# Token-major x for the modulation by DMA transposes in three batches, with a new order of all steps

## The chip, the cores and the metric

The kernel runs on one core of a Trainium2 chip. The core has five engines with an instruction queue each: TensorE (PE), VectorE (DVE), ScalarE (ACT), GpSimd (POOL) and SyncE (SP, which here only issues DMAs). Sixteen DMA engines move data between HBM and SBUF for the core. Every engine works through its own queue in order and waits for semaphores of the others. The metric is the device time of one execution in microseconds (us).

## The reference, cut to what matters

Eight batches of attention (8 heads, 576 tokens, head width 64) are followed by a token and channel mixing block (576 tokens, width 512):

```python
# attention: a pooled part and a banded part, summed
q_d, k_d, v_d = mean of 4 tokens each              # 144 pooled tokens
out_d = softmax(q_d @ k_d.T / 8) @ v_d             # repeated 4 times along the tokens
out_l = softmax(where(|i - j| < 4, q @ k.T / 8, -1e9)) @ v
x = out_up + out_l                                 # [8, 576, 512]
# mixing block
theta = x @ w_theta
zr, zi = x * cos(theta), x * sin(theta)
y = w_tok_r @ zr + w_tok_i @ zi                    # over the tokens
u = x + y
out = u + relu(u @ w_ch)
```

Inputs and outputs are float32; the kernel computes in bfloat16 with float32 sums.

## The kernel before, in words

Each stage of one batch is a Python generator; every `yield` ends a step. A letter stands for a generator, and three strings, `FIRST`, `PERIOD` (three times) and `LAST` (L695 to L708), give the order in which steps of all batches are issued: the letter says whose next step comes. `pin()` (L713) ties each engine's instructions to that order, so the strings fix the order in every queue. A step is written here as letter, batch and number from zero: A3.1 is the second `turns` step of batch 3.

- L, `load`: DMAs of q, k and v, 11 steps in batches 0 and 1 and 9 in the others (3 of q, 3 of k, 3 of v). They land in eight float32 buffers of tag `st`, taken in turn. The small l loads the weights, some of them into the same eight buffers.
- C, `cast`: float32 to bfloat16 into `q_tm`, `k_tm` (one buffer each) and `v_w`, in the order of the loads. In batch 0, DVE casts q, ACT casts k and POOL casts v (L216); in all other batches POOL casts all. The small c casts weights.
- A, `turns`: TensorE transposes q and k to `qT`, `kT`. From batch 2 on there are twelve steps of four matmuls (L329); steps 0 and 1 read what C wrote first, 2 and 3 what it wrote next, and so on: step n needs C step n // 2. ACT copies the result, DVE the pooled columns. The last step of A makes the pooled v (`vd`), with two multiplications on POOL (L362).
- S, `scores`: two steps for the pooled part, five for the band. ACT takes exponentials; from batch 1 on POOL zeroes what is off the band with two `affine_select` on each band step (L442, L444).
- N, V: products with v, pooled (three steps) and banded (five). T: five steps that transpose to `xT` with channels on partitions, and add both parts.
- H, `phases`: theta on TensorE, sine and cosine on ACT, five steps. M, `last_product`: the last 64 tokens on DVE.
- Z, `modulate`: for each of four chunks of 128 tokens, four TensorE transposes (L581) bring x to tokens on partitions in PSUM, and one DVE multiplication (L582) makes `z`. The fifth step does the last 64 tokens.
- X, `mix`: eight steps of nine matmuls (L608), with a DVE addition each (L612). U, `residuals`: u with tokens on partitions by four DMA transposes (L621) in batches 1 to 6. R, `channels`: the product with w_ch. O, `store`: the last addition, on DVE, and the DMA to HBM.
- W turns the token weights, D is a block of six matmuls whose result nobody reads (L282).

All DMAs of L, l, U and O (but one) are issued by SP, in the order of the strings; one that must wait for a buffer or for a result keeps all later ones waiting. One-bank PSUM tiles (`w1`) go round four buffers and two-bank ones (`w2`) round two.

Of the kernel before, what the change touches and what calls it, by code (L numbers as in the profile page):

```python
# [9 lines left out]
FP32 = mybir.dt.float32  # L10
BF16 = mybir.dt.bfloat16
# [6 lines left out]
H = 8  # L18
# [29 lines left out]
def kernel(  # L48
# [38 lines left out]
    def load(b):  # L87

        if b < WIDE:
            for hh in range(4):  # L90
                for nm, src in zip("qk", (q, k)):
                    nc.sync.dma_start(
                        out=stage(b, f"{nm}{hh}")[0:TR, 0:2 * NTR * D].rearrange("p (h e) -> p h e", h=2),
                        in_=src[b, 2 * hh:2 * hh + 2].rearrange("h (p r) d -> p h (r d)", r=NTR),
                    )
                    yield
        else:
            for nm, src in zip("qk", (q, k)):
                for i in range(3):
                    t = stage(b, f"{nm}{i}")[0:TR].rearrange("p (c h d) -> p c h d", c=2, d=D)  # L100
                    for j in range(2):
                        c = 2 * i + j
                        nc.sync.dma_start(
                            out=t[:, j], in_=src[b, :, TR * c:TR * c + TR, :].rearrange("h p d -> p h d"),
                        )
                    yield
        for i in range(3):
            t = stage(b, f"v{i}").rearrange("p (c h d) -> p c h d", c=2, d=D)
            for c in range(2 * i, min(2 * i + 2, NCH)):
                nc.sync.dma_start(  # L110
                    out=t[0:KW[c], c % 2],
                    in_=v[b, :, KS[c]:KS[c] + KW[c], :].rearrange("h p d -> p h d"),
                )
            yield

    def cast(b):

        q_tm = work.tile([TR, NTR, H, D], BF16, tag="q_tm", bufs=1, name=f"q_tm{b}")
        k_tm = work.tile([TR, NTR, H, D], BF16, tag="k_tm", bufs=1, name=f"k_tm{b}")
        v_w = v_ws[b % 2]  # L120
        inputs[b] = (q_tm, k_tm, v_w)
        eng = CASTS.get(b, CASTS[None])
        if b < WIDE:
            for hh in range(4):
                for i, dst in enumerate((q_tm, k_tm)):
                    eng[i](out=dst[:, :, 2 * hh:2 * hh + 2, :].rearrange("p r h d -> p h r d"),
                           in_=staged.pop((b, f"{'qk'[i]}{hh}"))[0:TR, 0:2 * NTR * D].rearrange(
                               "p (h r d) -> p h r d", h=2, d=D))
                    yield
        else:  # L130
            for i, dst in enumerate((q_tm, k_tm)):
                for c in range(3):
                    eng[i](out=dst[:, 2 * c:2 * c + 2].rearrange("p c h d -> p (c h d)"),  # L133
                           in_=staged.pop((b, f"{'qk'[i]}{c}"))[0:TR])
                    yield
        for i in range(3):
            t = staged.pop((b, f"v{i}")).rearrange("p (c h d) -> p c h d", c=2, d=D)
            n, rows = (2, P) if i < 2 else (1, KW[4])
            eng[2](out=v_w[0:rows, 2 * i:2 * i + n, :, 0:D], in_=t[0:rows, 0:n])  # L139
            yield  # L140
# [151 lines left out]
    def turns(b):  # L292
# [8 lines left out]
        def wide_turn(n, hh):  # L301
            tm, To = ((q_tm, qT), (k_tm, kT))[n]
            ps = w2(f"pstr{n}{hh}_{b}")
            for r in range(NTR):
                nc.tensor.matmul(
                    out=ps[:, r // 3, (r % 3) * TR:(r % 3) * TR + TR],
                    lhsT=tm[:, r, 2 * hh:2 * hh + 2, :], rhs=ip[:, 0:TR], start=True, stop=True,
                )
            (dve if n == 1 else act)(
                out=To[:, hh, :].rearrange("p (w k c) -> p w k c", k=2, c=3),  # L310
                in_=ps[:, :, 0:3 * TR].rearrange("p k (c w) -> p w k c", w=TR),
            )

            with nc.allow_low_precision(reason="sums are taken in float32 and rounded once"):
                if n == 0:
                    nc.vector.tensor_reduce(out=qdT[:, hh, :], in_=To[:, hh, :].rearrange("p (m j) -> p m j", j=4),
                           axis=AX.X, op=ALU.add)
                else:
                    nc.vector.tensor_reduce(out=kdP[:, hh, 0:4, 0:30],
                       in_=To[:, hh, 0:480].rearrange("p (g m j) -> p g m j", g=4, j=4),  # L320
                           axis=AX.X, op=ALU.add)
                    nc.vector.tensor_reduce(out=kdP[:, hh, 4, 0:24], in_=To[:, hh, 480:576].rearrange("p (m j) -> p m j", j=4),
                           axis=AX.X, op=ALU.add)

        def turn(n, c):
            tm, To = ((q_tm, qT), (k_tm, kT))[n]
            ps = w1(f"pstr{n}{c}_{b}")[:, 0:4 * TW].rearrange("p (hh w) -> p hh w", w=TW)
            for hh in range(4):
                nc.tensor.matmul(  # L329
                    out=ps[:, hh, :], lhsT=tm[:, c, 2 * hh:2 * hh + 2, :], rhs=ip, start=True, stop=True,  # L330
                )
            nc.scalar.copy(out=To[:, :, TR * c:TR * c + TR], in_=ps[:, :, 0:TR])  # L332
            if n == 0:
                dve(out=qdT[:, :, TP * c:TP * c + TP], in_=ps[:, :, TR:TW])
            elif c == 5:
                nc.scalar.copy(out=kdP[:, :, 4, 0:TP], in_=ps[:, :, TR:TW])
            else:
                for g in range(TP * c // 30, (TP * c + TP - 1) // 30 + 1):
                    lo, hi = max(TP * c, 30 * g), min(TP * c + TP, 30 * g + 30)
                    nc.scalar.copy(out=kdP[:, :, g, lo - 30 * g:hi - 30 * g],  # L340
                                   in_=ps[:, :, TR + lo - TP * c:TR + hi - TP * c])

        for i in range(8 if b < WIDE else 12):
            if b < WIDE:
                wide_turn(i % 2, i // 2)
            else:
                turn(i // 6, i % 6)
            yield
# [23 lines left out]
    def scores(b):  # L372
# [3 lines left out]
        pd = pds[b] = work.tile([P, H + 2, SD], BF16, tag="pd", name=f"pd{b}")  # L376
        pms[b] = []

        scale = SCL / 16.0 if b < WIDE else SCL

        def pooled_scores(dst, hh):
            for par in range(2):
# [152 lines left out]
            yield  # L535


    css = {}

    def phases(b):  # L540

# [24 lines left out]
    def last_product(b):  # L566
# [4 lines left out]
        )  # L571
        yield

    def modulate(b):

        xT = xTs[b]
        z = zs[b] = moep.tile([P, 9, DM], BF16, tag="z", name=f"z{b}")
        for c in range(4):
            x = w1(f"psxt{c}_{b}", BF16)[:, 0:DM].rearrange("p (e d) -> p e d", d=P)
            for dc in range(4):  # L580
                nc.tensor.transpose(out=x[:, dc, :], in_=xT[:, dc, P * c:P * c + P], identity=ident)  # L581
            nc.vector.tensor_tensor(  # L582
                out=z[:, 2 * c:2 * c + 2, :].rearrange("p r (e d) -> p r e d", d=P),
                in0=x.unsqueeze(1).to_broadcast([P, 2, 4, P]),
                in1=css.pop((b, c)).rearrange("p r (e d) -> p r e d", d=P), op=ALU.mult,
            )
# [80 lines left out]
    def store(b):  # L667
# [17 lines left out]
            yield  # L685


    DMA_U = (1, 2, 3, 4, 5, 6)

# [1 line left out]


    FIRST = (  # L695
        "LLLCCLCALLALLCCALACDLCLADACAlAlCSSSClCSLASlScDVlNCcNAlNlVcSDlLcccWcTCLTcVVLHTAZCLVCHTCWALWWWLLTLLCCA"
        "LCWZWAAHLLAHWHADLWCSLCCCMZCLLZASlZlLCXSXACANSAACXLCSLNAAAXNSSXVAccCAXTCALVAACVLXLSTTSSHLVVXLTLHCTZRO"
        "AHZZCLHVLROHRLLMCOCSZZCNRLROSLNALOA"
    )
    PERIOD = (  # L700
        "XSCSNTXCCAAXCUAAVAXUACVAXAVAAVXTSSTAXSTAUTHXULCNHZNCAHLZCVHHCZROLLSLMSZRLOZRORLOLROL"
    )
    PERIODS = 3
    LAST = (
        "ASXVAAAXAAVXACCNAVXAUTACCCSUTTXTASSCXAHXVZUNHCTHXCAUHZNHZSZLLLRCMOLARORSSCZLRSOOCCNAXAXACAVAAVXXAVTA"
        "XUSSTARVXSOSXASTTHVUXVTHUNHZUZHNZHRMOSSZRORZORVXSONXTVTXXTVHXVXUHTZXTZHZUUHXZHMURROZROOXXRORXOXXXXRO"
        "ROXRORORORO"
    )  # L708

    last = {}  # L710
# [13 lines left out]
    def batches(steps, bs=range(B)):  # L724
        for b in bs:
# [43 lines left out]
```

## Time and profile before

| | |
|---|---|
| median of 11 runs | 261.03 us (260.13 to 263.73) |
| the profiled execution | 261.55 us, its span 259.8 us |
| PE busy | 243.2 us of the span |
| DVE, ACT, POOL busy | 188.6, 178.7, 154.5 us |
| bytes moved | 46.73 MB, mean 180 GB/s |

The span goes from the first to the last instruction on the core. A line of the timeline or of the groups says start, length, engine, source line, operation and what it writes and reads; what stands in brackets is idle time before it and what ended it. In the slices a digit is the busy share of one fortieth of the span in tenths, 6.5 us a slice. The DMA share is the mean busy share of the sixteen DMA engines; overlapping packets can take it over 1. Durations of matmuls are modelled ends, so the cost of a matmul in a stream is read from the distance of the starts.

### The profile page before, as it was taken

What the parts mean: (1) busy time and instruction counts of PE and PEld (TensorE: products, weight loads), DVE (VectorE), ACT (ScalarE), POOL (GpSimd) and SP (SyncE); (2) the same over time, 40 slices, a digit from 0 to 9 for tenths busy, and PEclk for the clock granted to TensorE, in tenths of its full rate; (3) what the DMA queues carried; (4) which work ended last, traced back from release to release, by engine and by line L of the source; (5) the groups of instructions that cost most, each with busy time, mean ns of one, the idle gap of its engine ahead of it and who ended that gap; (6) DMA issues with size and microseconds to landing.
All of it is one profiled execution on the core that took longest, in us unless ns stands there. A gap on an engine that the chain in (4) does not pass through costs nothing.

```text
span 259.8 us, 7472 instructions
## 1 busy us (share of the span) xinstructions
PE 243.2 (94%) x2960; PEld 170.1 (65%) x2960; DVE 188.6 (73%) x421; ACT 178.7 (69%) x336; POOL 154.5 (59%) x178
## 2 busy tenths in 40 slices
PE   1869699999999999999999999999999999999993
PEld 1434466678657877588657866687668766776762
DVE  4865869956768777868696868785777588876443
ACT  3439378997889678956896779777886787334022
POOL 4244364489997979398748956798069762600000
PEclk9985679999999999999999999999999999999999
DMA  7999999999999951999789987898399032311324
GB/s 191 247 246 318 278 248 202 198 276 224 191 244 219 265 119 27 204 226 271 109 172 218 287 141 145 191 264 209 52 245 243 23 63 81 105 40 43 143 74 150
DMA packets 120851, 46.73 MB, mean 180 GB/s; under 512 B 110448, under 2 KB 114544, under 8 KB 120816
## 3 DMA queue, kind: packets, MB, share of 16 engines
q1 hardware_dynamic: 120736, 46.18, 80.7%
q8 instruction: 23, 0.38, 0.6%
q14 instruction: 12, 0.10, 0.1%
q10 hardware_dynamic: 80, 0.07, 0.1%
HBM read 33.65 MB, written 9.44 MB: 166 GB/s over the span
## 4 chain that ended last, share of the span: by engine, by line
PE 85%; ACT 5%; DVE 5%; DMA 2%; issue 1%; SPq 0%; DVEq 0%
PE psu L608 27%; PE psr L632 11%; PE psth L546 10%; PE pstr L329 6%; PE psS L421 4%; PE psloc L498 4%; PE wu L282 3%; PE psxt L581 3%; PE xTps L528 3%; DMA st_k<-in_k_dram 2%; PE psnd L460 2%; PE psr L650 2%; PE pstl L557 1%; ACT pm L429 1%; PE psnd L466 1%; PE psxd L483 1%
## 5 line engine op out<-in xcount | busy, mean ns | idle before, releaser
L608 PE MATMUL psu<-WT,z 128*128 128x288 bf16 x576 | 80.0, 286 | 0.0
L608 PEld LDWEIGHTS <-z 128*128 128x128 bf16 x576 | 53.6, 98 | 15.2 <-issue 0.8
L442 POOL TENSOR_SCALAR_AFFINE_SELECT pm<-pm 128x1024 bf16<-128x1024 bf16 (+1 forms) x35 | 36.7, 1047 | 22.9 <-ACT pm L429 22.8
L612 DVE TENSOR_TENSOR uT<-psu,xT 128x288 bf16<-128x288 f32 x64 | 29.2, 456 | 24.2 <-PE psu L608 23.3
L429 ACT ACTIVATE pm<-psS 128x1024 bf16<-128x1024 f32 (+1 forms) x40 | 38.1, 984 | 10.7 <-PE psS L421 10.5
L444 POOL TENSOR_SCALAR_AFFINE_SELECT pm<-pm 128x1024 bf16<-128x1024 bf16 (+1 forms) x35 | 36.7, 1049 | 2.4
L546 PE MATMUL psth<-wth,xT 128*128 128x512 bf16 x128 | 32.9, 379 | 0.4 <-DVE xT L529 0.4
L632 PE MATMUL psr<-wch,uT 128*128 128x512 bf16 x128 | 32.0, 380 | 0.0
L551 ACT ACTIVATE cs<-psth,pihc 128x512 bf16<-128x512 f32 x32 | 22.0, 688 | 11.8 <-PE psth L546 8.0
L529 DVE TENSOR_TENSOR xT<-xTps,xdT 128x480 bf16<-128x480 bf16 (+1 forms) x40 | 24.9, 631 | 5.8 <-PE xTps L528 5.2
L507 DVE TENSOR_TENSOR tmp<-psloc,rl 120x512 bf16<-120x512 f32 (+1 forms) x40 | 27.6, 690 | 1.4
L139 POOL CAST v_w<-st_v 128x1024 bf16<-128x1024 f32 (+1 forms) x24 | 20.8, 897 | 11.3 <-DMA st_v<-in_v_dram 11.3
L582 DVE TENSOR_TENSOR z<-psxt,cs 128x1024 bf16<-128x1024 bf16 x32 | 21.7, 685 | 4.7 <-PE psxt L581 3.1
L133 POOL CAST k_tm<-st_k 96x1024 bf16<-96x1024 f32 x18 | 18.8, 1045 | 8.8 <-DMA st_k<-in_k_dram 8.2
L332 ACT CAST kT<-pstr 128x384 bf16<-128x384 f32 x36 | 18.0, 500 | 7.0 <-PE pstr L329 6.9
L662 ACT ACTIVATE rel<-psr 128x512 f32<-128x512 f32 (+1 forms) x16 | 7.9, 492 | 18.5 <-PE psr L650 15.0
L133 POOL CAST q_tm<-st_q 96x1024 bf16<-96x1024 f32 x18 | 18.4, 1035 | 1.9 <-DMA st_q<-in_q_dram 1.9
L332 ACT CAST qT<-pstr 128x384 bf16<-128x384 f32 x36 | 16.0, 481 | 4.9 <-PE pstr L329 4.7
L552 ACT ACTIVATE cs<-psth 128x512 bf16<-128x512 f32 x32 | 18.9, 590 | 0.0
L673 DVE SCALAR_TENSOR_TENSOR osb<-psr,utm 128x512 f32<-128x512 f32 x24 | 16.3, 687 | 2.4 <-PE psr L632 1.9
L632 PEld LDWEIGHTS <-uT 128*128 128x128 bf16 x128 | 11.2, 98 | 9.8
L498 PE MATMUL psloc<-v_w,pm 128*128 128x65 bf16 (+1 forms) x320 | 17.3, 198 | 0.0
(107 smaller groups left out, 439.5 us busy)
## 6 DMA issues: line engine op xcount, KB each, us to landing
st_v<-in_v_dram SPq DMA_DIRECT2D x32, 256.0 KB, 5.2
out_dram<-osb SPq DMA_DIRECT2D x32, 256.0 KB, 3.7
st_q<-in_q_dram SPq DMA_DIRECT2D x36, 192.0 KB, 4.8
st_k<-in_k_dram SPq DMA_DIRECT2D x36, 192.0 KB, 3.9
st_q<-in_q_dram SPq DMA_DIRECT2D x8, 288.0 KB, 6.0
st_k<-in_k_dram SPq DMA_DIRECT2D x8, 288.0 KB, 11.3
st_v<-in_v_dram SPq DMA_DIRECT2D x8, 200.0 KB
w<-in_moe_w_tok_r_dram SPq DMA_DIRECT2D x2, 576.0 KB
```

What stands on the lines that cost most here:

```text
L133: eng[i](out=dst[:, 2 * c:2 * c + 2].rearrange("p c h d -> p (c h d)"), in_=staged.pop((b, f"{'qk'[i]}{c}"))[0:TR])
L332: nc.scalar.copy(out=To[:, :, TR * c:TR * c + TR], in_=ps[:, :, 0:TR])
L429: nc.scalar.activation(out=pv, in_=ps[0:kw].rearrange("p e (j w) -> p (e j) w", w=P)[:, :, 0:qn], func=AF.Exp, scale=SCL,)
L442: nc.gpsimd.affine_select(out=pv, in_=pv, compare_op=ALU.is_ge, fill=0.0, base=off, pattern=[[0, 8], [-1, qn]], channel_multiplier=1)
L444: nc.gpsimd.affine_select(out=pv, in_=pv, compare_op=ALU.is_ge, fill=0.0, base=6 - off, pattern=[[0, 8], [1, qn]], channel_multiplier=-1)
L498: nc.tensor.matmul(out=pv[0:qn, par, j, :], lhsT=pms[b][c][0:kw, 4 * par + j, 0:qn], rhs=v_w[0:kw, c, 2 * j + par, 0:65], start=(j == 0), ...
L507: nc.vector.tensor_tensor(out=tmp[0:cnt].rearrange("p (j e d) -> p e j d", e=2, j=4), in0=pv[0:cnt, :, :, 0:D], in1=rl[0:cnt].unsqueeze(3) ...
L529: nc.vector.tensor_tensor(out=xT[:, :, QS[c]:QS[c] + cnt].rearrange("p e (m j) -> p e m j", j=4), in0=ps[:, :, 0:cnt].rearrange("p e (m j) ...
L546: nc.tensor.matmul(out=th, lhsT=xT[:, dc, P * c:P * c + P], rhs=wth[:, dc, :], start=(dc == 0), stop=(dc == 3),)
L608: nc.tensor.matmul(out=ps[:, 0:288], lhsT=z[:, j, P * dc:P * dc + P], rhs=WT[:, j, cols], start=(j == 0), stop=(j == 8),)
L612: nc.vector.tensor_tensor(out=uT[:, dc, cols], in0=ps[:, 0:288], in1=xT[:, dc, cols], op=ALU.add)
L632: nc.tensor.matmul(out=psr, lhsT=uT[:, dc, P * c:P * c + P], rhs=wch[:, dc, :], start=(dc == 0), stop=(dc == 3),)
```

## The change

In batches 5, 6 and 7, four DMA transposes a batch, issued by SP in a new step Y (`tokens`), write x with tokens on partitions to SBUF, and Z's first four steps multiply from there; their sixteen TensorE transposes a batch are gone. Y reads `xT` after T's last step. The buffer `x_tm` is there once, so Y of a batch waits for Z of the one before.

All three order strings are new. In `LAST` twelve Y steps are added. The number of steps in each section changes a little: `FIRST` has two C, one L and one S more and one N less, `LAST` the reverse. The strings also move the five D blocks, the weight loads and the loads of batch 1.

A second part of the diff, for turning q and k by DMA in batches of a list `DMA_A`, is off: that list is empty, and with it those lines do what they did before. The only trace of it is that `q_tm` and `k_tm` have 128 partitions in place of 96.

```diff
+    def tokens(b):
+
+        x = x_tm[b] = moep.tile([P, 4, 4, P], BF16, tag="xtm", bufs=1, name=f"xtm_{b}")
+        for dc in range(4):
+            nc.sync.dma_start_transpose(out=x[:, dc], in_=xTs[b][:, dc, 0:512])
+            yield
+
     def modulate(b):
 
         xT = xTs[b]
         z = zs[b] = moep.tile([P, 9, DM], BF16, tag="z", name=f"z{b}")
         for c in range(4):
-            x = w1(f"psxt{c}_{b}", BF16)[:, 0:DM].rearrange("p (e d) -> p e d", d=P)
-            for dc in range(4):
-                nc.tensor.transpose(out=x[:, dc, :], in_=xT[:, dc, P * c:P * c + P], identity=ident)
+            if b in DMA_X:
+                x = x_tm[b][:, :, c, :]
+            else:
+                x = w1(f"psxt{c}_{b}", BF16)[:, 0:DM].rearrange("p (e d) -> p e d", d=P)
+                for dc in range(4):
+                    nc.tensor.transpose(out=x[:, dc, :], in_=xT[:, dc, P * c:P * c + P], identity=ident)
             nc.vector.tensor_tensor(
...
-    DMA_U = (1, 2, 3, 4, 5, 6)
+    DMA_A, DMA_X, DMA_U = (), (5, 6, 7), (1, 2, 3, 4, 5, 6)
...
     FIRST = (
-        "LLLCCLCALLALLCCALACDLCLADACAlAlCSSSClCSLASlScDVlNCcNAlNlVcSDlLcccWcTCLTcVVLHTAZCLVCHTCWALWWWLLTLLCCA"
-        "LCWZWAAHLLAHWHADLWCSLCCCMZCLLZASlZlLCXSXACANSAACXLCSLNAAAXNSSXVAccCAXTCALVAACVLXLSTTSSHLVVXLTLHCTZRO"
-        "AHZZCLHVLROHRLLMCOCSZZCNRLROSLNALOA"
+        "LLLCCCLLAALLCCLLLAALAlClCCLLCAALLAlSCSlSCSlSAllLScCCVlDcVCLCSLcALNALcDDcCALcWcVDcNDAALWWCCLWWCLAAWSL"
+        "WALNWWLTCSCCVSlVTACSTSTHTLVNHNZHZHCZHNZLMCAAALAZAALCLlVCCASCCCTLXAXVAXAAACXTSLSXTASSXVLCALcAHVTNcHXT"
+        "LLHZHZCVHRCLZOLCSXMRRLLLSOOSZZCROLRCLO"
     )
     PERIOD = (
-        "XSCSNTXCCAAXCUAAVAXUACVAXAVAAVXTSSTAXSTAUTHXULCNHZNCAHLZCVHHCZROLLSLMSZRLOZRORLOLROL"
+        "SCNAAAXAVAXAXAAVCNVUCXCAAXASCSLUTTXATSSTCXAHVUXVTHUNZZHHRCLCOZLHMSSZRROLCOLZRLLLROLO"
     )
     PERIODS = 3
     LAST = (
-        "ASXVAAAXAAVXACCNAVXAUTACCCSUTTXTASSCXAHXVZUNHCTHXCAUHZNHZSZLLLRCMOLARORSSCZLRSOOCCNAXAXACAVAAVXXAVTA"
-        "XUSSTARVXSOSXASTTHVUXVTHUNHZUZHNZHRMOSSZRORZORVXSONXTVTXXTVHXVXUHTZXTZHZUUHXZHMURROZROOXXRORXOXXXXRO"
-        "ROXRORORORO"
+        "CAVAAASXCAVAANXACVAAXNSTCVAUTSCTTASSCXTYAANYSUYAAXAYSNHHXVVXAVZAHZNLUCCLHXUZHCMLZAVAASCZRLROOAXSCTXT"
+        "SSTTRVOAXSSTRYRYOUSOYNXYNXVVNXSHVVXZHXTHTTZHVHTZHRHUUUOZTYHRYRMYYOZOROXXRXOUXZZHHZZUMXXXZXXXXXRUUOXX"
+        "RXOROROROXRORROROROO"
     )
...
-                     M=batches(last_product), U=batches(residuals, DMA_U),
+                     M=batches(last_product), Y=batches(tokens, DMA_X), U=batches(residuals, DMA_U),
```

More of the change, by code (lines that the diff above doesn't have):

```diff
@@ L98, in load @@
             for nm, src in zip("qk", (q, k)):
+                rows = P if b in DMA_A else TR
                 for i in range(3):
[L100 to L105, printed above, removed]
+                    t = stage(b, f"{nm}{i}").rearrange("p (c h d) -> p c h d", c=2, d=D)
+                    for c in range(2 * i, 2 * i + 2):
+                        n = min(rows, S - rows * c)
+                        if n > 0:
+                            nc.sync.dma_start(
+                                out=t[0:n, c % 2], in_=src[b, :, rows * c:rows * c + n, :].rearrange("h p d -> p h d"),
+                            )
                     yield
@@ L116, in cast @@
     def cast(b):
-        q_tm = work.tile([TR, NTR, H, D], BF16, tag="q_tm", bufs=1, name=f"q_tm{b}")
-        k_tm = work.tile([TR, NTR, H, D], BF16, tag="k_tm", bufs=1, name=f"k_tm{b}")
+        q_tm = work.tile([P, NTR, H, D], BF16, tag="q_tm", bufs=1, name=f"q_tm{b}")
+        k_tm = work.tile([P, NTR, H, D], BF16, tag="k_tm", bufs=1, name=f"k_tm{b}")
         v_w = v_ws[b % 2]
@@ L125, in cast @@
                 for i, dst in enumerate((q_tm, k_tm)):
-                    eng[i](out=dst[:, :, 2 * hh:2 * hh + 2, :].rearrange("p r h d -> p h r d"),
+                    eng[i](out=dst[0:TR, :, 2 * hh:2 * hh + 2, :].rearrange("p r h d -> p h r d"),
                            in_=staged.pop((b, f"{'qk'[i]}{hh}"))[0:TR, 0:2 * NTR * D].rearrange(
@@ L132, in cast @@
                 for c in range(3):
-                    eng[i](out=dst[:, 2 * c:2 * c + 2].rearrange("p c h d -> p (c h d)"),
-                           in_=staged.pop((b, f"{'qk'[i]}{c}"))[0:TR])
+                    rows, n = (TR, 2) if b not in DMA_A else (P, 2) if c < 2 else (HALF, 1)
+                    eng[i](out=dst[0:rows, 2 * c:2 * c + n].rearrange("p c h d -> p (c h d)"),
+                           in_=staged.pop((b, f"{'qk'[i]}{c}"))[0:rows, 0:n * H * D])
                     yield
@@ L306, in wide_turn @@
                     out=ps[:, r // 3, (r % 3) * TR:(r % 3) * TR + TR],
-                    lhsT=tm[:, r, 2 * hh:2 * hh + 2, :], rhs=ip[:, 0:TR], start=True, stop=True,
+                    lhsT=tm[0:TR, r, 2 * hh:2 * hh + 2, :], rhs=ip[:, 0:TR], start=True, stop=True,
                 )
@@ L329, in turn @@
                 nc.tensor.matmul(
-                    out=ps[:, hh, :], lhsT=tm[:, c, 2 * hh:2 * hh + 2, :], rhs=ip, start=True, stop=True,
+                    out=ps[:, hh, :], lhsT=tm[0:TR, c, 2 * hh:2 * hh + 2, :], rhs=ip, start=True, stop=True,
                 )
@@ L341, in turn, with dma_turn @@
                                    in_=ps[:, :, TR + lo - TP * c:TR + hi - TP * c])
+        def dma_turn(n, c):
+            tm, To = ((q_tm, qT), (k_tm, kT))[n]
+            if c < 5:
+                rows = min(P, S - P * c)
+                nc.sync.dma_start_transpose(out=To[:, :, P * c:P * c + rows],
+                                            in_=tm[0:rows, c].rearrange("p h d -> p (h d)"))
+                return
+            x = To.rearrange("p e (m j) -> p e m j", j=4)
+            t = stg.tile([P, 1024], FP32, tag="st", name=f"sum{n}_{b}")[:, 0:4 * SD].rearrange("p (e m) -> p e m", m=SD)
+            add = nc.gpsimd.tensor_tensor
+            add(out=t, in0=x[:, :, :, 0], in1=x[:, :, :, 1], op=ALU.add)
+            add(out=t, in0=t, in1=x[:, :, :, 2], op=ALU.add)
+            if n == 0:
+                add(out=qdT, in0=t, in1=x[:, :, :, 3], op=ALU.add)
+            else:
+                add(out=kdP[:, :, 0:4, 0:30], in0=t[:, :, 0:120].rearrange("p e (g m) -> p e g m", g=4),
+                    in1=x[:, :, 0:120, 3].rearrange("p e (g m) -> p e g m", g=4), op=ALU.add)
+                add(out=kdP[:, :, 4, 0:24], in0=t[:, :, 120:SD], in1=x[:, :, 120:SD, 3], op=ALU.add)
         for i in range(8 if b < WIDE else 12):
-            if b < WIDE:
+            if b in DMA_A:
+                dma_turn(i // 6, i % 6)
+            elif b < WIDE:
                 wide_turn(i % 2, i // 2)
@@ L377, in scores @@
         pms[b] = []
-        scale = SCL / 16.0 if b < WIDE else SCL
+        scale = SCL / 16.0 if b < WIDE or b in DMA_A else SCL
         def pooled_scores(dst, hh):
@@ L535, in transposes @@
             yield
-    css = {}
+    css, x_tm = {}, {}
     def phases(b):
@@ L578, in modulate @@
         for c in range(4):
-            x = w1(f"psxt{c}_{b}", BF16)[:, 0:DM].rearrange("p (e d) -> p e d", d=P)
-            for dc in range(4):
-                nc.tensor.transpose(out=x[:, dc, :], in_=xT[:, dc, P * c:P * c + P], identity=ident)
+            if b in DMA_X:
+                x = x_tm[b][:, :, c, :]
+            else:
+                x = w1(f"psxt{c}_{b}", BF16)[:, 0:DM].rearrange("p (e d) -> p e d", d=P)
+                for dc in range(4):
+                    nc.tensor.transpose(out=x[:, dc, :], in_=xT[:, dc, P * c:P * c + P], identity=ident)
             nc.vector.tensor_tensor(
```

## The prediction

> **What bounds the kernel now.** I read the slices first, then the windows of the head, then POOL's timeline. The page:
>
> ```profile
> span 259.8 us, 7472 instructions
> ...
> PE   1869699999999999999999999999999999999993
> ...
> POOL 4244364489997979398748956798069762600000
> ...
> DMA  7999999999999951999789987898399032311324
> ```
>
> PE has no idle slice from about 45 us to the end, so every us of PE work taken out after that is a us of time. But the DMA engines too are full until slice 14, and the head decides when PE gets its work. By windows (columns: PE, PEld, DVE, ACT, POOL busy, clock, DMA share, GB/s):
>
> ```profile
> 30.00:47.00 17.00, 16.06 (x175) 10.57 (x173) 14.16 (x28) 13.92 (x22) 8.44 (x10) 0.85 1.10 221
> 47.00:60.00 13.00, 12.98 (x190) 9.29 (x186) 9.07 (x24) 12.15 (x23) 8.95 (x11) 1.00 1.12 246
> 60.00:70.00 10.00, 9.90 (x152) 7.64 (x149) 7.02 (x16) 8.05 (x19) 9.79 (x11) 1.00 1.16 207
> 70.00:83.80 13.80, 13.71 (x171) 8.93 (x169) 10.72 (x21) 12.29 (x21) 12.38 (x14) 1.00 1.12 223
> ```
>
> The DMA share is over 1 throughout, and from 54 us POOL too is full. POOL's timeline shows where it waits for a load and what each of its operations costs from start to start:
>
> ```profile
> 44.97 1.04 POOL L139 CAST v_w<-st_v 128x1024 bf16<-128x1024 f32 x1 [1.70 <-DMA st_v<-in_v_dram]
> 46.39 0.61 POOL L139 CAST v_w<-st_v 100x512 bf16<-100x512 f32 x1 [0.38 <-DMA st_v<-in_v_dram]
> 48.21 1.04 POOL L133 CAST q_tm<-st_q 96x1024 bf16<-96x1024 f32 x1 [1.20 <-DMA st_q<-in_q_dram]
> 49.94 1.04 POOL L133 CAST q_tm<-st_q 96x1024 bf16<-96x1024 f32 x1 [0.69 <-DMA st_q<-in_q_dram]
> 53.00 1.18 POOL L362 TENSOR_TENSOR vd<-last,own 128x256 bf16<-128x256 bf16 x2 [2.02 <-ACT last L360]
> 54.12 1.03 POOL L133 CAST q_tm<-st_q 96x1024 bf16<-96x1024 f32 x1
> 55.11 1.09 POOL L442 TENSOR_SCALAR_AFFINE_SELECT pm<-pm 128x1024 bf16<-128x1024 bf16 x1
> 56.27 1.09 POOL L444 TENSOR_SCALAR_AFFINE_SELECT pm<-pm 128x1024 bf16<-128x1024 bf16 x1
> 57.31 1.03 POOL L133 CAST k_tm<-st_k 96x1024 bf16<-96x1024 f32 x1
> ```
>
> POOL waits for the last v of batch 1 until 46.39 and is through at 47.0 (C1.10). A cast costs 1.0, the pair of selects of a band step 2.2 (55.11 to 57.31), vd 1.1.
>
> [...] four of L581 take 0.22 us between the starts around them. [...] L569, both inputs in SBUF, takes 0.91 at worst, 0.425 at the median. [...] The lines for what is moved:
>
> ```profile
> L621 SPq DMA_TRANSPOSE utm<-uT x24: 1190/1220/2420, 92.3 to 236.4; - x24
> DMA to landing us min/median/max: 2.3/2.8/4.7
> L582 DVE TENSOR_TENSOR z<-psxt,cs x32: 676/690/693, 39.6 to 236.3; 128x1024 bf16<-128x1024 bf16 x32
> L569 DVE TENSOR_TENSOR zl<-csl,xT x8: 411/425/908, 49.5 to 237.4; 128x512 bf16<-128x512 bf16 x8
> ```
>
> **The removed transposes.** 12 Z steps of four matmuls at 0.22 us: 2.64 us of PE work, all where PE is full. This is the whole direct gain. Nothing else is removed.
>
> **The added transposes.** Twelve on SP at 1.22 us of issue, the last landing 2.8 us after its issue starts: a batch's four need 3 x 1.22 + 2.8 = 6.5 us from T's last addition. In the new order of PE, Z's first step comes 8.5, 9.5 and 8.8 us of PE work after T's last step (batches 5, 6, 7). In batch 5 one U stands among the Ys (7.7 us against 8.5, less about 0.7 for T's addition), in batch 6 two stores and one U: tight but hidden behind S, X, A and V steps. I take 0; if all cover failed, half a us to one and a half a batch. DVE's 12 multiplications now read SBUF twice: 0.69 again (the 0.425 of L569 is for half the size[...]), and in batch 5, where POOL still works, up to 1.05 (a select) more each: 0 to 2 us of DVE, whose steps there, from X4.1 to C7.7, sum to 16.4 us beside 18.9 of PE. I take 0, hidden by the rest; with the cover gone 1 us.
>
> **The new order, head.** PE prices of the steps, from the distances of starts in its timeline: A 0.21 (0.26 in batches 0 and 1, last step 0.39); S 0.20, 0.39, then 0.33, 0.23, 0.28, 0.23, 0.25; N 0.50, 0.50, 0.27; V 0.24; T 0.21; H 0.86, last 0.47; Z 0.22, last 0.35; X 1.10; R 0.86 (1.08 in batches 0 and 7), last 0.67; W 0.45. Summed over the strings without D: 216.05 before, 213.41 after. From 72 us on the kernel before spends 182 us for 176 us of these, a factor of 1.033.
>
> All bytes needed before C1.10 are the same set in both orders (batches 0 and 1 and three weights, 10.9 MB), and the DMA side is full all that time, so C1.10 stays at 47.0, although D no longer delays A0.4 to A0.7 (which frees DVE some 2 us sooner: it only waits longer for batch 1). After it, POOL's new order is: S1.2, vd of A1.8, C2.0, S1.3, S1.4, C2.1 to C2.5, S1.5, C2.6 to C2.8, C3.0, S1.6, vd of A2.12, S2.2, C3.1. That is five full band steps (11.0), the short one (1.8), two vd (2.2), eight q and k casts (8.0), three v casts (2.6): 25.6, so C3.1 ends at 72.6 without a wait. One wait is to be seen: S1.5's exponential stands on ACT behind H0. From S1.4's end at 50.3 (47.0, then A1.8's copies and two exponentials): two table loads at 1.28, H0 at 4 x 1.17 + 0.85, six A2 copies at 0.42, one at 0.62, the exponential 0.93: 12.2, so 62.4, where POOL is free at 60.7. With it C3.1 ends at 74.3.
>
> PE's order needs C3.1 much earlier than it did. X0.0 stands behind A2.6, which needs C2.3, on POOL's list at 58.7; X0.0 starts near 59.7 (51.4 before), and A3.1, which needs C3.1, is reached 10.4 us of work later, at 70.4. There PE stops for 2.2 to 3.9 us, and behind A3.1 in its queue wait H1, N2, X0.6, and so all of ACT's and DVE's next work. At A3.1 the new order has 35.0 us of PE work done. The kernel before had 39.6 done at 72.6 and 41.0 at 74.3. Deficit 4.6 to 6.0, less the 2.64 saved: 2.0 to 3.4 us of work, times 1.033: 2.0 to 3.5. I take the middle, 2.8, since helpers ahead after the stop may win back some of the 0.6 us that PE loses between 74 and 84 before. Periods: same work, same 27.4 us; 0 to 0.4 us each either way.
>
> Sum on the profiled execution: 259.8 + 2.8 = 262.6 of span, 261.55 + 2.8 = 264.4; on the median of 261.03, which lies 0.5 lower, 263.8.
>
> **Rivals.** (1) Faster: loads are queued earlier now (theta, token weights and the first q and k of batch 1 stand ahead of S0), so if the DMA side had slack that its share hides, C1.10 comes earlier and so the whole POOL chain. For: in the windows from 28 to 36 us it moved 0.21 to 0.27 MB/us, and 0.36 when weights ran. Against: share over 1 throughout. The point from which it decides: the time is equal when A3.1 starts at 70.6 (before had 35.0 + 2.64 done then), so C1.10 must come 2 to 4 us earlier; the full saving needs C3.1 near 68, and gives 258.3. (2) No change: the chain runs 2 us ahead of my sum, PE is never stopped, and the late X0.0 eats just the saved 2.64: 261. (3) Slower by the tail: the transposes land late because SP, in order, waits for a store between them; DVE then waits in Z, and X behind it: 1 us a batch on top of the stop, 266.5. For: batch 5 has under 1 us of margin; against: 2 us in the others. That the change does nothing is no rival for Y; for the q and k part it is so by its empty list.
>
> **How the numbers follow.** The stop in the head, tail hidden: 0.52, 262.3 to 265.5, and 263.8 the likeliest. Rival 3: 0.14. Rival 2: 0.16. Rival 1: 0.18. Half a per cent (1.3 us) is about what a measurement of this kernel tells from none. Slower 0.66, same 0.16, faster 0.18. The range goes from 259.2, which leaves out most of rival 1, to 267.0.
>
> **What would show it.** PE idle of 2 us or more before the A3.1 matmuls of `q_tm` between 70 and 75 us, released by POOL's cast; X0.0 at 58 to 61; C1.10 ending at 46 to 48; PE free of L581 in the last three batches; DVE waits before Z under 0.5 us. Wrong would be: C1.10 before 45, periods that are not 27.4 us, or DVE waiting in Z for a transpose.

## The result, and the profile after

The changed kernel takes 265.38 us (median of 12 executions, 263.43 to 270.98) against 260.89 us of the kernel before (47 executions, 259.36 to 264.3); the ratio, which like all ratios below takes only the executions within 1.5% of each kernel's fastest, is 1.014 with an interval of 1.0109 to 1.0171. The change makes the kernel slower, by 1.4%. The profiled execution took 267.68 us, its span 266.0 us, 2.3 us above the median; its mean clock of PE was 0.971, where the twelve have 0.964 to 0.993 and a median of 0.976 (the clock is looked at below).

The page of the changed kernel, the same rows as of the kernel before:

```profile
span 266.0 us, 7391 instructions
...
PE   1369569998999999999999999999999999999993
...
POOL 4245425597698697939683978399965881000000
PEclk9999996579999999999999999999999999999998
DMA  7999997999998898399957996799689244375145
```

PE has its last idle slice (an 8) at 60 to 66 us, where before it had none from 33 us on. The clock's three low digits stand at 40 to 60 us; before they stood at 13 to 39 us. The windows of the head (PE, PEld, DVE, ACT, POOL busy, clock, DMA share, GB/s):

```profile
30.00:47.00 17.00, 11.63 (x128) 7.80 (x124) 8.57 (x17) 9.68 (x15) 7.93 (x9) 0.86 1.00 219
47.00:60.00 13.00, 12.59 (x137) 7.72 (x132) 8.69 (x20) 9.58 (x15) 9.66 (x12) 0.66 1.23 216
60.00:70.00 10.00, 8.83 (x134) 7.21 (x132) 7.98 (x19) 8.82 (x22) 6.05 (x7) 1.00 1.14 225
70.00:83.80 13.80, 13.80 (x183) 10.09 (x181) 8.24 (x20) 11.57 (x23) 13.66 (x16) 1.00 1.18 197
```

From 30 to 47 us PE is busy for 11.6 us where it was for 16.1; ACT for 9.7 where it was for 13.9. From 47 to 60 us PE is busy, but at 0.66 of its clock. What PE waited for from 26 to 66 us (total, times, longest), first in the kernel before, then after:

```profile
PE psnd L460 <- DVE tmp L507: 1.7, 1, 1.7
PE wps L269 <- DVE xT L529: 0.4, 1, 0.4
PE psth L546 <- DVE xT L529: 0.4, 1, 0.4
PE pstr L305 <- DVE xd L473: 0.2, 1, 0.2
```

```profile
PE wps L272 <- POOL wtm L256: 2.7, 2, 1.4
PE pstr L308 <- POOL q_tm L128: 2.2, 2, 1.8
PE pszl L627 <- DVE qdT L337: 0.9, 1, 0.9
PE pstr L308 <- DVE tmp L532: 0.6, 1, 0.6
PE wps L272 <- POOL wtm L258: 0.3, 1, 0.3
...
```

Two waits are new: W.0 for POOL's casts of the token weights, and A1.4 for the cast C1.4 of a load of batch 1. POOL's timeline says why, and where it waits itself:

```profile
38.68 0.82 POOL L128 CAST q_tm<-st_q 96x768 bf16<-96x768 f32 x1 [4.92 <-DMA st_q<-in_q_dram]
...
47.78 0.61 POOL L142 CAST v_w<-st_v 100x512 bf16<-100x512 f32 x1 [0.51 <-DMA st_v<-in_v_dram]
51.02 1.09 POOL L467 TENSOR_SCALAR_AFFINE_SELECT pm<-pm 128x1024 bf16<-128x1024 bf16 x1 [2.62 <-ACT pm L454]
52.18 1.09 POOL L469 TENSOR_SCALAR_AFFINE_SELECT pm<-pm 128x1024 bf16<-128x1024 bf16 x1
53.24 1.18 POOL L387 TENSOR_TENSOR vd<-last,own 128x256 bf16<-128x256 bf16 x2
...
61.71 3.20 POOL L136 CAST k_tm<-st_k 96x1024 bf16<-96x1024 f32 x3
68.79 1.09 POOL L467 TENSOR_SCALAR_AFFINE_SELECT pm<-pm 128x1024 bf16<-128x1024 bf16 x1 [3.88 <-ACT pm L454]
```

C1.4 (the line at 38.68) waited 4.9 us for its load, C1.10 ended at 48.4, S1.2's select began only at 51.0, after 2.6 us of waiting for its exponential, and S1.5's waited 3.9 us more. X0.0 started on PE at 66.1 us (51.4 before).

The DMA transposes and what reads them, by the tile `xtm`:

```profile
L603 SPq DMA_TRANSPOSE xtm<-xT x12: 1204/1264/2281, 186.9 to 234.2; - x12
L617 DVE TENSOR_TENSOR z<-xtm,cs x12: 678/684/860, 196.2 to 240.0; 128x1024 bf16<-128x1024 bf16 x12
its engine sat idle before it (us, times) until:
  ACT cs L577: 0.3, 1
...
DMA to landing us min/median/max: 2.5/3.0/3.4
```

DVE never waited for a transpose: its one idle time ahead of these multiplications, 0.3 us, was for a sine on ACT. PE shows no wait of 0.2 us or more from 176 us to the end.

So the loss lies in the head. A measure shows it: take a step of X, the start of DVE's addition for it, and subtract the PE work that the order puts ahead of this addition (the step's own nine matmuls included), at the prices of the prediction (D counted as nothing). The difference, the lag, grows where PE waits, works on D, or has half its clock, and by some 3% of all work.

| lag at, us | before | after | difference |
|---|---|---|---|
| X0.3 | 32.06 | 41.76 | +9.70 |
| X1.0 (first period) | 34.11 | 42.84 | +8.73 |
| X4.0 (LAST) | 37.25 | 45.37 | +8.12 |
| end of the span | 43.78 | 52.55 | +8.77 |
| work in all | 216.05 | 213.41 | -2.64 |

8.77 - 2.64 = 6.13, the difference of the spans (266.0 - 259.8 = 6.2) up to rounding. All of the loss is there at X0.3. From X1.0 to the end both kernels gain the same lag (9.67 and 9.71), so PERIOD and LAST together gain the 2.64 us of transposes taken out, in these two executions. More time at half clock is not the reason: by the record the clock stood at half for 13.6 us ahead of X0.3 before, and for 13.7 after.

### The profile page after: what moved, and what is told of

Its sections match the earlier page's. It is cut to its first block, busy times and chain, and to the rows that moved or that the text cites. A ratio compares the mean times of both kernels' runs of the same rounds, so it can differ in the third digit from the quotient of the medians.

```text
span 266.0 us, 7391 instructions
## 1 busy us (share of the span) xinstructions
PE 242.3 (91%) x2912; PEld 171.1 (64%) x2912; DVE 186.4 (70%) x421; ACT 177.0 (67%) x334; POOL 153.7 (58%) x178
## 4 chain that ended last, share of the span: by engine, by line
PE 79%; DMA 12%; DVE 4%; ACT 1%; SPq 1%; POOL 1%; issue 1%; DVEq 0%; POOLq 0%
PE psu L643 27%; PE psr L667 11%; PE psth L571 10%; DMA st_q<-in_q_dram 6%; PE pstr L332 5%; DMA w<-in_moe_w_tok_r_dram 4%; PE xTps L553 4%; PE psloc L523 4%; PE psS L446 4%; DMA st_v<-in_v_dram 2%; PE psxt L616 2%; PE psnd L485 2%; PE psr L685 1%; PE psnd L491 1%; PE psSd L408 1%; PE pszl L627 1%
## 5 line engine op out<-in xcount | busy, mean ns | idle before, releaser
L142 POOL CAST v_w<-st_v 128x1024 bf16<-128x1024 f32 (+1 forms) x24 | 21.1, 896 | 13.7 <-DMA st_v<-in_v_dram 13.6
L667 PEld LDWEIGHTS <-uT 128*128 128x128 bf16 x128 | 11.6, 98 | 10.9
L523 PEld LDWEIGHTS <-pm 128*128 128x128 bf16 (+1 forms) x320 | 15.6, 107 | 3.4 <-issue 0.5
```

Source lines behind the costliest of these rows:

```text
L523: nc.tensor.matmul(out=pv[0:qn, par, j, :], lhsT=pms[b][c][0:kw, 4 * par + j, 0:qn], rhs=v_w[0:kw, c, 2 * j + par, 0:65], start=(j == 0), ...
L667: nc.tensor.matmul(out=psr, lhsT=uT[:, dc, P * c:P * c + P], rhs=wch[:, dc, :], start=(dc == 0), stop=(dc == 3),)
```

## The experiments

All times are medians. The kernel before took 260.93 us beside the runs of the table of two by two and the first run on batch 0, 261.2 beside the second run on batch 0 and the three with another number of D, 260.97 beside those on the loads and on L7.5, and 261.15 beside the last. Several of the edits below are shown as lists of steps and not as the strings that the file has.

**Two heads by two ways to transpose.** The first run takes the new order with TensorE transposes:

```diff
-    DMA_A, DMA_X, DMA_U = (), (5, 6, 7), (1, 2, 3, 4, 5, 6)
+    DMA_A, DMA_X, DMA_U = (), (), (1, 2, 3, 4, 5, 6)
     LAST = (   # its twelve Y left out
```

> The changed kernel with its new order, but the modulation of batches 5, 6 and 7 again from TensorE transposes and no Y steps. Theory H (the head of the new order costs all, and the DMA transposes give what they should): PE has 2.64 us more work where it is full, so 2.7 us longer than the changed kernel: 268.1 us. Theory T (the transposes by DMA cost as much in SP, DVE and waits as they save): the same as the changed kernel, 265.4 us, or less.

The second takes the order of the kernel before for FIRST:

```diff
     FIRST = (
-        "LLLCCCLLAALLCC ... RLLLSOOSZZCROLRCLO"
+        "LLLCCLCALLALLC ... CNRLROSLALOA" "CSLC"   # FIRST of before, last N left to PERIOD
     )
```

> FIRST of the kernel before (its last N left to PERIOD, and one C, S, L and C more at its end, so that the counts fit), with PERIOD, LAST and the DMA transposes of the changed kernel. Theory H: the loss of the head is gone and the saving of 2.64 us of PE work, times 1.03, is left: 258.3 us, 0.990 of the kernel before. Theory T, or a loss in the new PERIOD or LAST: 262 to 265 us. X0.0 should start at 51 us again, and PE should run at the full clock from 45 us.

The third does both.

> As the run with the old head, but with TensorE transposes in all batches and no Y. With the other three this makes a table of two heads by two ways to transpose. Theory H: 261.0 us, equal to the kernel before, so that the new PERIOD and LAST in themselves are worth nothing, and 2.7 us above the run with DMA transposes. If the new LAST by itself costs time, over 262; if it by itself gains, under 260.

| | new head | old head |
|---|---|---|
| TensorE transposes | 270.49 (1.033) | 266.91 (1.021) |
| DMA transposes | 265.38 (1.014) | 261.62 (0.998) |

In brackets the ratio to the kernel before, which is not the quotient of the medians: of the second run 12 of 20 executions lie over 1.5% above its fastest, 257.59 us, and by the medians of all it is at 1.003. The intervals are 1.0242 to 1.0413 and 1.0143 to 1.027 in the first row, 1.0109 to 1.0171 and 0.9942 to 1.0019 in the second. The head costs 3.6 to 3.8 us in either row (1.2% and 1.6%, or 3.1 and 4.2 us, by the ratios). The DMA transposes gain 5.1 to 5.3 us in either column (4.9 and 6.0 by the ratios), twice what theory H had and what theory T denied: in the new LAST, with Z where it now stands, TensorE transposes cost more than their work. In the profiles of the first and the third run PE stops five times from 176 us on, for 1.9 us in all, among these 1.1 us for sines and 0.6 us for Z's multiplications; in that of the changed kernel it has no such stop. The lag grows in LAST by 9.80 and 9.82 us with them (first and third run) and by 7.18 and 7.33 with the DMA (the changed kernel and the second run), against 6.53 in the old LAST with TensorE transposes. So against the old LAST the new one gives 2.64 - 0.65 to 0.8, about 1.9 us, in these executions; the new PERIOD adds 0.6 (its three turns gain 2.53 us of lag in these four runs, 3.14 in the kernel before). No run has the DMA transposes in the old LAST, so what they are worth there was not measured. Theory T falls. Theory H holds for the head, but the second run did not come out at 258.3: old head and DMA transposes together only equal the kernel before. Where the rest went is taken up with the last three runs.

**Batch 0 into the hole.** From 26 to 40 us PE was busy 8.96 us (11.67 before), ACT 4.58 (8.21), DVE 7.87 (10.78). In the old head T0.0 to T0.3, H0.0, H0.1 and Z0.0 run there, in the new one they stand behind the steps of batch 1. Two runs moved such steps ahead:

```diff
-  ... W.0 V0.2 D.3 N0.1 D.4 A1.3 A1.4 ... N0.2 ... T0.0 ... V0.3 S1.2 V0.4 T0.1 A1.8 S1.3 T0.2 S1.4 T0.3 H0.0 T0.4 ... H0.1
+  ... W.0 V0.2 D.3 N0.1 D.4 N0.2 T0.0 V0.3 T0.1 V0.4 T0.2 H0.0 T0.3 H0.1 T0.4 A1.3 A1.4 ... S1.2 A1.8 S1.3 S1.4
```

> The changed kernel with ten steps of batch 0 (N0.2, T0.0 to T0.4, V0.3, V0.4, H0.0, H0.1), whose data is there, moved ahead of A1.3, which waits until 39.5 us for a load. Theory P (PE idles at 34 to 47 us because work of batch 0 stands behind steps of batch 1 that wait for loads): some 3.8 us of PE work done in that idle time, X0.0 near 62 instead of 66 us, 261.5 to 262.5 us. Theory L (the later loads and casts of batch 1 set the head): under 1 us back, 264.5 to 265.4.

```diff
-  ... D.1 D.2 A1.2 ...
+  ... D.1 D.2 V0.2 N0.1 N0.2 T0.0 V0.3 T0.1 H0.0 T0.2 V0.4 H0.1 T0.3 Z0.0 H0.2 T0.4 Z0.1 H0.3 H0.4 A1.2 ...
```

> The changed kernel with the theta, sine and cosine of batch 0 and what they need (V0.2 to V0.4, N0.1, N0.2, T0, H0, Z0.0, Z0.1) ahead of A1.2 and of the three weight casts on ACT, where ACT is idle for 7 us. Theory P2 (these steps stand between S1.4 and S1.5 on ACT, and make POOL wait 3.9 us for S1.5's exponential and PE wait for A2's copies): POOL's wait is gone, X0.0 at 60 to 62 us instead of 66.1, and 260 to 261.5 us. Theory L (the order of the loads sets the head): X0.0 at 65 or later, 264.5 us or more.

They took 270.01 us (1.0325, interval 1.0267 to 1.0384) and 275.23 us (1.055, 1.0502 to 1.0598). Both expectations fall, with the wrong sign. POOL's first select of batch 1, in the first and then in the second of these runs:

```profile
54.84 1.09 POOL L467 TENSOR_SCALAR_AFFINE_SELECT pm<-pm 128x1024 bf16<-128x1024 bf16 x1 [5.83 <-ACT pm L454]
```

```profile
58.37 1.09 POOL L467 TENSOR_SCALAR_AFFINE_SELECT pm<-pm 128x1024 bf16<-128x1024 bf16 x1 [11.56 <-ACT pm L454]
```

The steps of batch 0 are a chain from PE to DVE to PE to ACT. Put in one block, they hold PE at each link, and A1.3 and A1.2, which have their data, wait behind them (in the second run A1.2 came at 44.0 instead of 29.8 us). So S1.2 is later, and POOL waits 5.8 and 11.6 us for its exponential instead of 2.6. This shows when X0.0 comes in the new order, in all runs with it (us; the runs on D and on the loads are told below):

| run | POOL's first select of batch 1 | X0.0 on PE | distance |
|---|---|---|---|
| changed kernel | 51.02 | 66.11 | 15.1 |
| new order, TensorE transposes | 48.49 | 61.62 | 13.1 |
| ten steps of batch 0 ahead | 54.84 | 67.98 | 13.1 |
| phases of batch 0 ahead | 58.37 | 72.54 | 14.2 |
| five more D | 49.56 | 62.69 | 13.1 |
| no D | 49.97 | 65.06 | 15.1 |
| new order, old loads | 54.60 | 68.72 | 14.1 |
| before | 55.11 | 51.39 | -3.7 |
| old head, DMA transposes | 51.61 | 47.68 | -3.9 |

That three runs have 13.1, two 15.1 and one 14.1 is no chance. It looks as if C2.3 set X0.0, by way of A2.6, but PE never waits for C2.3: A2.6 starts 0.3 us after its end in the three runs with 13.1, and 0.8 to 2.5 us after it in the other four. PE's last wait ahead of X0.0 is at Z0.4, which reads `zl`, the product that DVE makes in M0. In the changed kernel:

```profile
62.81 1.20 DVE L594 TENSOR_TENSOR zl<-csl,xT 128x512 bf16<-128x512 bf16 x1
64.06 0.42 PEld L627 LDWEIGHTS <-zl 128*64 128x64 bf16 x8 [0.91 <-DVE zl L594]
65.25 0.37 PE L332 MATMUL pstr<-ip,k_tm 96*128 96x120 bf16 x4
```

Both inputs of this product lie in SBUF. Here it lasts 0.63 to 1.30 us in the seven runs with the new order, against 0.42 at the median, and in each of them it ends 0.27 or 0.28 us after the end of the POOL operation that was under way when it started. The profile of the kernel before has the same: the product that took 0.91 us started at 78.84 and ended at 79.75, and the cast of q that POOL began at 78.44 ended at 79.47. In the three runs with 13.1 this operation is the cast C2.2, in the one with 14.1 C2.3, in the two with 15.1 C2.4: the distances differ by one cast each. In these six runs X0.0 then starts 2.10 us after the end of `zl`. So X0.0 moves by whole casts of POOL, though PE stands still for only 0.3 to 0.9 us at Z0.4. Which cast it is depends on when `zl` can start, and ahead of it stand H0 on PE, its sines on ACT, and Z0.3. The seventh run (phases ahead) has this end of `zl` too, but PE waits 2.1 us for a cast of q instead. The old order puts X0.0 ahead of all this, so that it doesn't matter there.

**The clock.** In these profiles the record of the clock holds only 1 and 0.5. In the profile of the changed kernel it is at 0.5 from 42.3 us for 13.7 us, in that of the kernel before from 18.0 for 6.8 and from 28.3 for 6.8 us. Two runs change D:

```diff
-    WARM = 5
+    WARM = 10     # two D ahead of W.0, two ahead of A1.4, one ahead of A1.5
```

> The changed kernel with five more D blocks (two ahead of W.0, two ahead of A1.4, one ahead of A1.5), put where PE waited 2.3 us for the casts of the token weights and 2.3 us for a load of batch 1. Theory K (PE's idle time at 32 to 40 us sends its clock to half for one to four windows of 3.4 us between 42 and 56 us, just where PE has work again): the clock stays full there, mean clock 0.987 or more in each run, median 263.4 us as in the runs of the changed kernel with one window. Theory O (the order alone, the clock is no cause): 265.4 us, or more by what D delays.

```diff
-    WARM = 5
+    WARM = 0      # all D left out of FIRST
```

> The changed kernel without any D block. Theory K: the clock comes up later and falls more often, 266.5 to 268.5 us. If D costs PE more than the clock gives: under 264.5 us.

With ten D the clock stays full, as expected:

```profile
span 263.5 us, 7451 instructions
...
PEclk9999999999999999999999999999999999999999
```

Its mean was 0.994 to 1.000 in all four executions (0.964 to 0.993 in those of the changed kernel). Yet the median is 266.01 us (1.0199, 1.0156 to 1.0242), not below 265.38. Theory K is right on what D does to the clock and wrong on its worth. Single executions of the changed kernel do differ by the clock: those with a mean of 0.993 had spans of 261.7 to 262.1 us, those at 0.97 to 0.971 of 263.0 to 266.3. With ten D and nearly the same clock the four spans are 263.5 to 265.1 us, so a part of the 6.5 us of further D seems to have stood in PE's way. But the kernel before has such stretches too. Compared at one short stretch each, the lag at X0.3 is 37.27 in the new order (with TensorE transposes) and 28.56 in the old (with DMA transposes): 8.7 apart, nearly the 9.70 of the two profiles. And at a mean clock of 0.993 in both, the kernel before has spans of 257.3 to 259.3 us (14 executions beside the experiments), so that some 3 us remain. So the clock makes much of the scatter, and, as far as three executions of the changed kernel can show, no more than a third of the difference of 4.5. Without any D: 267.39 us (1.0252, 1.0207 to 1.0298), 2 us more than with five.

**The loads.** In the new order four loads of batch 1 go ahead of the token weights. Two runs exchange the order of these loads and of their casts, once in the old head and once in the new, with no other move than a few places for W.0 and C1.4 or for A1.1 and A1.2, as that needs:

```diff
-  SP: th0 th1 tok0 L1.0 tok1 tok2 tok3 tok4 tok5 L1.1 L1.2 L1.3 L1.4 ...
+  SP: th0 th1 L1.0 L1.1 L1.2 L1.3 tok0 tok1 tok2 tok3 tok4 L1.4 tok5 ...   # old head; casts alike
```

> The kernel with the old head, new PERIOD and LAST and the DMA transposes, with the loads of weights and of batch 1 and their casts in the order of the changed kernel (four loads of batch 1 ahead of the token weights; W.0 and C1.4 moved by a few places, as the new order needs), all else in the old order. Theory D (this order of loads makes the new head's loss): DVE's first addition of X0 at 55 us or later instead of 49 to 53, and 3 to 5 us more than with the old loads, 264.5 to 266.5 us. Theory S (the order of the steps on PE, ACT and DVE makes it): 261 to 263 us.

> The changed kernel with the loads of weights and of batch 1 and their casts in the order of the kernel before (A1.1 and A1.2 moved by a few places, as that needs), all else unchanged. Theory D: DVE's first addition of X0 at 61 us or earlier (67.4 in the profile of the changed kernel, 64.0 with its clock full), 261 to 262.5 us. Theory S: 264 to 266 us, X0 hardly earlier.

The old head goes from 261.62 to 263.95 us (1.0077, 1.0045 to 1.0108): 2.3 us, less than theory D had and more than theory S. (X0's first addition came at 57.9 us in its profile, as theory D had it, but this profile is of one of its longer executions.) The new head goes from 265.38 to 268.78 (1.0287, 1.0225 to 1.035): 3.4 us the wrong way for theory D, and more than S allowed. So neither the loads nor the order of steps is the cause by itself: each order of steps is faster with its own loads. What remains is that with the new loads the old order of steps is 1.4 us better than the new one, and with the old loads 7.2 us.

**The tail.** The second run's profile had 257.59 us, near 258.3, but its median was 261.62. One more run filled two waits of its head with D:

```diff
-    WARM = 5
+    WARM = 7      # one D more ahead of S0.0, one ahead of A1.1
```

> The kernel with the old head, new PERIOD and LAST and the DMA transposes, with two more D blocks, ahead of S0.0 and of A1.1, where PE waited 2.5 and 2.1 us. Theory K: the windows of half clock that take its median from 257.6 (its profiled execution, mean clock 0.991) to 261.6 us are gone: 258 us, 0.989 of the kernel before. If these windows come from elsewhere: 261 to 262 us.

262.01 us (1.0002, 0.9974 to 1.0029): nothing gained, so K falls here too. But its profile shows a stop in the tail that the one of the second run does not have. PE's longest wait in LAST, then SP's and POOL's rows that make it:

```profile
PE pstr L332 <- POOL k_tm L136: 2.1, 1, 2.1
```

```profile
180.23 3.76 SPq L603 DMA_TRANSPOSE xtm<-xT  x2
184.04 1.26 SPq L656 DMA_TRANSPOSE utm<-uT  x1
185.34 2.57 SPq L603 DMA_TRANSPOSE xtm<-xT  x2
188.01 1.10 SPq L105 DMA_DIRECT2D st_k<-in_k_dram  x2
```

```profile
193.33 1.53 POOL L136 CAST k_tm<-st_k 96x1024 bf16<-96x1024 f32 x1 [3.50 <-DMA st_k<-in_k_dram]
```

Y5.0 to Y5.3 and one U keep SP busy from 180.2 to 187.9 us, and the load L7.5 is queued behind them. It lands late, POOL waits 3.5 us for it, and A7.10, which needs this cast, stops PE for 2.1 us. POOL waits for this load in all nine profiles with L7.5 behind Y5, 1.2 to 3.5 us, and PE stops in the four of them where that wait is over 2.0 us, for 0.2 to 2.1 us (0.9 with ten D); in the changed kernel POOL waits 1.5 us and PE not at all. The next run exchanges two entries of SP's queue:

```diff
-    Y5.1  U4.1  Y5.2  Y5.3  L7.5  U4.2
+    Y5.1  L7.5  Y5.2  Y5.3  U4.1  U4.2
```

> The kernel with the old head, new PERIOD and LAST and the DMA transposes, with two steps of SP's order exchanged: the load L7.5 goes to the place of U4.1, ahead of Y5.2 and Y5.3, and U4.1 to its place. Theory Q (in LAST the four Y steps of batch 5 keep SP busy for 5 us and more, so that L7.5 is issued late, POOL's cast of it ends late, and PE stops 0.9 to 2.1 us at A7.10 in most executions): no PE wait at A7.10, 1.5 to 2 us less than without the exchange, 259.5 to 260.2 us, 0.995 of the kernel before or less. If the load is not what A7.10 waits for: 261.6 us as without the exchange.

In its profile L7.5 is issued at 183.1 us, and neither POOL waits for it nor PE at A7.10; the same holds for the last run below, which has the exchange too. So L7.5 behind Y5 makes this wait. The median is 261.68 us (1.0023, 0.9989 to 1.0056), the same as without: the stop is not there in most executions (five of the nine profiles have none), or something else takes its place. In all profiles with the patched old head the lag grows by 4.0 to 5.7 us from X0.3 to X1.0, where it grows by 2.05 in the kernel before, and PE's longest wait there is this one (of the run with L7.5 ahead):

```profile
PE psnd L485 <- ACT pm L454: 1.3, 1, 1.3
```

It is N2.1, which in the patched order stands behind S2.5 and S2.6 and needs, as they do, one of two two-bank buffers. The clock fell to half for 3.4 us around it in four of these five. The last run keeps the exchange of L7.5 and moves N2.1 behind A3.2 to A3.4 and X1.0, in the first period alone:

```diff
-    "SCNAAAXAVAXAX ..."      # first PERIOD
+    "SCAAAXNAVAXAX ..."
```

> The run with the old head and L7.5 ahead of Y5.2, with one more exchange where FIRST meets the first PERIOD: N2.1 stands behind A3.2 to A3.4 and X1.0 instead of directly behind S2.6. In the runs with the old head PE waited 1.3 us there for S2.5's exponential to free a two-bank buffer, and its clock fell to half for 3.4 us after it. Theory J (this junction, made by the patch of the old head, hides the saving of the DMA transposes): no wait at N2.1, no half clock near 83 us, the lag between X0.3 and X1.0 grows by 2.0 us as in the kernel before and not by 4.0 to 5.7, 258.3 to 259.3 us, 0.990 to 0.994 of the kernel before. Theory R (the saving is lost elsewhere): 261 us or more.

260.86 us against 261.15 (0.9976, 0.9951 to 1.0001). The wait and the half clock at 83 us are gone from its profile, but the lag still grows by 4.07 us between X0.3 and X1.0, so the patch costs some 2 us elsewhere at this junction. It has the lowest median of the kernels with the DMA transposes, though by its ratio it is level with the second run (0.998); that it is faster than the kernel before is not shown, and a gain would be 0.3 to 0.6 us, not 2.

## Why the prediction was right or wrong

**The direction and the size** came out near: 263.8 with a range of 259.2 to 267.0, measured 265.38. But two steps of the working were wrong and others were mis-sized, and the place of the loss was another. The nearness of the size is in part luck: the stop on which the sum rested is not there, and a larger loss that the sum did not have stands in its place.

**The removed transposes**: right as to the work, 2.64 us less. The step did not see that where the new LAST puts Z, TensorE transposes would have cost 5.1 to 5.3 us; the same lag from X1.0 to the end as before is the sum of 0.6 us gained in PERIOD and as much lost in LAST.

**The added transposes**: right as far as they went. Landing took 2.5 to 3.4 us (2.3 to 4.7 had been seen), DVE's multiplications 0.684 at the median and 0.86 at most, and no wait in Z. The allowance of up to 1.05 us more for each of them in batch 5 was an estimate, the length of a select; the two that started under a POOL cast took 0.77 and 0.86 us. What the step left out is the other side of SP's queue: it asked whether the transposes would be late, not what stands behind them. L7.5 does, and in four of nine profiles that costs PE 0.2 to 2.1 us.

**C1.10 at 47.0, because the DMA side is full**: 48.4. The bytes are the same, but the full side hid a hole: from 40 to 47 us the share was 0.82 and the rate 169 GB/s (1.04 and 201 before).

**POOL's chain without a wait from C1.10 to C2.3**: the first mis-sized step. The chain starts at S1.2's select, and I took S1.2's exponential as ready. It was 2.6 us late, since PE came to S1.2 only at 49.3 us. With C1.10's 1.4 that makes C2.3 end at 62.8 instead of 58.7, 4.0 of the 6.4 us by which X0.0 is later than forecast (59.7, measured 66.1); the other 2.4 come after it, at Z0.4 and what stands ahead of it. The wait for S1.5, further down the list, was 3.9 us instead of 1.7.

**X0.0 behind A2.6, which needs C2.3**: wrong as to what holds PE. C2.3 was done at 62.8 us and A2.6 started at 65.25; in none of the seven kernels with the new order does PE wait for C2.3. PE's last wait ahead of X0.0 is at Z0.4, for `zl`, which ends just after a POOL cast. The prediction had read the worst case of this product, 0.91 us, off the profile of before, but did not look for it in the head.

**A3.1 needs C3.1 and stops PE at 70.4**: wrong. This is the step that failed, since the forecast loss rests on it. By the rule that stands in the text on the kernel, step n needs C step n // 2, so A3.1 needs C3.0, which was done at 74.5 in time for A3.0 at 76.6. There is no wait there. What took its place lies earlier: PE had 12.5 us of work done at 47 us where the kernel before had 17.5, having waited for W.0's and A1.4's casts, and lost more until X0.0. The deficit at 72 us was 8.7 us, not 4.6 to 6.0.

**The clock**: the prices were taken at full clock. It was at half from 42.3 to 55.9 us, and H0.0 took 1.71 instead of 0.86. The runs show that this adds to the scatter of both kernels; with the clock full throughout (ten D) the ratio is still 1.02.

**Periods**: 27.4 forecast; from X2.0 to X3.0 27.20 (27.37 before). Right.

**The rivals**: the faster one is refuted by C1.10, which came later. No change had one thing right, that PE is not stopped at A3.1, but its chain was to run 2 us ahead of the sum, and X0.0 came 6.4 us behind it. The slower tail was nearest in its time, 266.5, and wrong in its mechanism: nothing waited in Z.

What stays open: why the new order of steps is 3.4 us worse with the old loads than with the new ones, and which of its many moves makes the head slower. Two moves of one block each made it worse, and no run took a single move back.

## What to carry to other kernels

Where a step is moved behind the output of a slow engine's chain, find what starts the chain and price the wait for that too, back to the engine that feeds it; here the chain began with the first exponential, which was 2.6 us late. Then check that the chain is the last thing awaited: here C2.3 ended before PE got to A2.6, and another wait, one step earlier, held PE. When DMAs are added to an in-order queue, look at what is queued behind them and who needs it, not only at when they land themselves. In a head in which five engines are interleaved by hand, a block moved into a hole can bring its own chain of waits along: both blocks that were moved here did.

## What the hardware showed that was not expected

In the head the clock fell to half though no gap between matmuls ahead of it was over 1.8 us. In the two profiles of the kernel before and the changed kernel it fell at 18.0 and 28.3 us (before) and at 42.3 us (changed) and stayed at half for 6.8, 6.8 and 13.7 us. In the 6.8 us ahead of these falls the longest gap between matmuls was 1.2, 1.7 and 1.8 us, and PE was busy for 73%, 74% and 71% of the time. With ten D the row of the clock shows no fall. How much idle time sends it to half was not shown.

The clock row shows 9 for the time before the record starts, which here is not full speed: in the changed kernel the record starts at 25.2 us, the D at 21.5 took 2.55 us for six matmuls and the one at 28.5 took 1.30. Without any D the record started at 55.6 us, a W step took 0.71 instead of 0.45 us until then, and the whole kernel lost only 2 us. From this one run the estimate is that PE at half its speed costs little where it waits for loads anyway; that the work of the five D was gone too was not measured apart.

A DVE product with both inputs in SBUF took longer while POOL worked: in the seven runs with the new order `zl` of batch 0 took 0.63 to 1.30 us instead of 0.42 and ended 0.27 or 0.28 us after the end of a POOL operation, and the POOL cast after that took 1.22 or 1.23 us instead of 1.04. In six of these runs X0.0 started 2.10 us after the end of `zl`, so it moved in steps of a cast, 1.0 us.
